# Loading the first two blocks of each rest chain earlier and thinner, with their tables built at twice the rate

## The chip, the cores and the metric

The kernel runs on one core of a Trainium2 chip. A core has a tensor engine (PE, with its weight loads shown apart as PEld), a vector engine (DVE), a scalar engine (ACT), GpSimd (POOL) and a sync engine (SP) that here does almost nothing but issue DMA transfers. Each engine works through its own list of instructions in order; semaphores hold one back for another. The metric is the time of one execution on the device in microseconds (us).

## The reference

`x` is 8 sequences of 5056 rows with 128 channels. First every channel of every sequence is convolved (linearly, along the rows) with a filter `h` of the same length, by real Fourier transforms of twice the length:

```python
Xf = np.fft.rfft(x, n=2*S, axis=1); Hf = np.fft.rfft(h, n=2*S, axis=0)
y = np.fft.irfft(Xf * Hf[None], n=2*S, axis=1)[:, :S, :]
```

The 40448 rows of the result are then the tokens of a mixture of 16 experts. A token's group is the largest of 4 group logits, its expert the largest of 4 logits in that group, and its weight is the product of the two softmax values. It goes through that expert alone:

```python
h = np.maximum(xg[mask_e] @ w1[g, e], 0.0)      # 128 -> 1024
out[tok_idx] = combined[:, None] * (h @ w2[g, e])   # 1024 -> 128
```

## The kernel before, in words

The convolution runs in three rounds over the sequences (`stage1`, `groups`, `side`), and the routed rows are scattered by expert into a table `srt` in DRAM. The experts then work on blocks of 512 rows of one expert. The first 59 blocks (`NW_MIN` = 59, numbered from 0) surely exist whatever the data, so they are written out without a branch: the plain blocks. Block 34 (`NA`) is the first for which all of the routing is known. What is left of each expert after that, the rest, depends on the data: some further blocks of 512 rows, then a chain of blocks of 384 rows (numbered from `T0` = 1000) and a chain of 256 rows (from `H0` = 2000), each block behind a branch.

One block is 8 steps. A step `k` of the plain blocks (k = 8 x block + step, 472 steps in all) has three matmuls of the first layer (`mm1`, L1400 to L1402: products of the high and low parts, into the PSUM tiles `px`/`aux`), a Relu on ACT (L1405), the low part of the hidden rows on DVE (L1406, `h0l` to `h3l`), and three matmuls of the second layer for an earlier step (L1418 to L1420). Between these lie the splits of the next block's weights and rows into high and low parts (`split`, ACT L1340 and DVE L1341), the turning of the next rows (L1356) and of the output (`out_turn`, L1459, up to block 51). Each split of the next block begins at step 4 of a block with the first half of its first weights, `w0h`.

The order of instructions is the order of the Python calls. For each step the loop in `run` calls `advance` on a few generators (a side chain's next piece) and then adds the step itself. Three of these matter here:

- `table_b` builds the three small tables that the rest needs (row and expert of each block): tens of DVE operations on 128x16 numbers, each piece ending in a `yield`, and for each table one store to DRAM (`tabd`, L1113) and one load back (`tabr`, L1118). It begins at step 272 (8 x `NA`).
- `fill_rows` writes 16 stretches of empty rows into `srt` (L1196), one every fourth step from step 284 on.
- `ffn_ahead` loads the first two blocks of each of the two chains, and then splits the first block's rows and weights into tiles of their own:

```python
for j in (T0, T0 + 1, H0, H0 + 1):
    yield from self.ffn_xs(j)          # four loads of rows (L1304), one of ids
    for q in (0, 2):
        self.ffn_w(j, (q,))            # one load of 512 KB of weights (L1333)
        yield
for j in (T0, H0):
    for q in ("x", 0, 1, 2) if j == T0 else ("x", 0, 1):
        self.keep_first(j, q)          # one split: ACT and DVE
        yield
        yield
```

So it has 28 pieces that issue a transfer and 14 that hold seven splits.

All of these transfers go through SP in program order, between the plain blocks' own: block j's step 0 issues the rows of block j+2 (L1304, four loads and the ids), step 2 its two weight loads (L1333), step 1 is followed by the store of the previous block's output (`outd`, L1460), and step 5 reads that output back row by row into the tile `xt` (`out_back`, L1465), which POOL then multiplies by the rows' weights (`weigh`, L1489, at step 1 of the next block) and scatters to the output (L1533). There is one such `xt` tile, so the read has to wait until POOL has weighed the rows before. `take` (L1465 too) reads back halves of outputs that earlier blocks had put aside.

Of the kernel before, what the change touches and what calls it, by code (L numbers as in the profile page):

```python
# [38 lines left out]
NW_MIN = NC  # L39
# [15 lines left out]
START1, END0 = 26, 24  # L55
NTA = 7
FILL, EMPTY = 12, 256
AHEAD = 52
RP = 3
PRE = 40  # L60
LOAD1 = 14
# [176 lines left out]
class Kernel:  # L238
# [1506 lines left out]
    def run(self):  # L1745
        tc = self.tc
        with ExitStack() as ctx:
            self.pools(ctx)
            with ExitStack() as c2:
# [10 lines left out]
                def add(f, w=0.0, ends=False):  # L1760
                    main.append((w, f, ends))
# [4 lines left out]
                def advance(g):  # L1766
                    return lambda: next(g, None)
# [47 lines left out]
                ta, tq, tb, fill = self.table_a(), self.table_c(), self.table_b(), self.fill_rows()  # L1815
                ahead = self.ffn_ahead()
                steps = [f for j in range(NW_MIN) for f in self.ffn_steps(j, (BLK, None) if j else None, NW_MAX)]
                for k, f in enumerate(steps):
                    for g in rest[LATE * k:LATE * k + LATE]:
                        add(g)  # L1820
                    if k == 8 * (N0 - 2) - SIDE1:
                        mark["end", 1] = len(main)
                    if k == START2 - 7:
                        add(lambda: [side[2][0](q) for q in range(len(SIDE_AT))])
                    if k == START2:
                        mark["start", 2] = len(main)
                    if 8 * (N0 - 2) - SIDE1 < k:
                        for _ in range(NTA):
                            add(advance(ta))
                    if k == 8 * (NA - 2) - SIDE2:  # L1830
                        mark["end", 2] = len(main)
                    if 8 * (NA - 2) - SIDE2 < k < 8 * NA:
                        for _ in range(NTA):
                            add(advance(tq))
                    if 8 * NA <= k:
                        add(advance(tb))
                    if 8 * NA + FILL <= k and k % 4 == 3:
                        add(advance(fill))
                    if 8 * NW_MIN - AHEAD <= k:
                        add(advance(ahead))  # L1840
                    if k < 4:
                        add(lambda q=(0, 2, 1, 3)[k]: self.ffn_w(1, (q,)))
                    add(f, FW[k % 8])
                    if k in (8 * (N0 - 2) - 1, 8 * (NA - 2) - 1):
                        add(self.drain)
                    elif k < 8 * (NA - 2) and k % 8 not in (3, 4, 5, 6):
                        add(lambda: self.send("s"))
                    elif k >= 8 * (NA - 2) and k % 8 in (7, 0, 1, 2):
                        add(lambda: self.scatter_out(1, True))
                    if k % 8 == 6:  # L1850
                        add(self.more_due)
                    m, n = k // 8 - NA, (PUT1 - PUT0) // 2
                    if k % 8 == 3 and 0 <= m < TAKE and (m + 1) * n // TAKE > m * n // TAKE:
                        add(lambda i=m * n // TAKE: self.take(i))
# [32 lines left out]
```

## Time and profile before

| | |
|---|---|
| runs before | 1615.23, 1625.37, 1626.6 us; median 1625.37 us |
| the profiled execution | 1622.21 us, its span 1620.5 us |
| granted PE clock over the span | 0.997 |
| busy: PE, DVE, ACT, POOL | 96%, 82%, 62%, 51% |
| DMA moved | 345.88 MB, 213 GB/s in the mean |

The span runs from the first to the last instruction that the profile shows; the run's time holds 1.7 us more. A busy share is a mean over the whole span, which has very different stages; the stage of this change is the part from about 1060 us (step 272) to 1340 us (end of the plain blocks). DVE and ACT intervals may overlap a little with the next one, since instructions are pipelined, so what an operation costs its engine is read from the distance of two starts.

### The profile page before, as it was taken

The page shows a single profiled execution, that of the slowest core. Times are in us where ns is not written, and L with a number is a line of the kernel's source. Part 1 is how long each engine was busy: PE and PEld are TensorE (multiplying, and loading weights), DVE is VectorE, ACT ScalarE, POOL GpSimd, SP SyncE. Part 2 cuts the span into 40 slices and gives each one's busy share as a digit, 9 for nine tenths or more (in the row PEclk, how much of TensorE's full clock was granted, in tenths as well). Part 3 has the DMA queues.
Part 4 walks back from the last instruction along what each step waited for, and adds up shares of the span by engine and source line. Part 5 has one row for each costly group of instructions (what it writes and reads, how often), then busy time and mean ns, then how long its engine had stood idle before and what let it go on. Part 6 is the DMA issues. An engine that isn't in the chain of part 4 may idle for free. (4 is left out here: it accounts for less than half of the span.)

```text
span 1620.5 us, 47337 instructions
## 1 busy us (share of the span) xinstructions
PE 1559.0 (96%) x16248; PEld 1217.5 (75%) x16248; DVE 1322.4 (82%) x2817; ACT 1001.6 (62%) x2240; POOL 827.3 (51%) x812
## 2 busy tenths in 40 slices
PE   8998999998899989999999999999999999999997
PEld 8676855557766647887777777788888877888997
DVE  6554699885698987888888889999998988887887
ACT  5565544444455546666666666677776777666775
POOL 1453234343375663155655666355777866234444
PEclk9999999999999999999999999999999999999999
DMA  7797879889799988667787757677888996555666
GB/s 213 217 293 241 229 230 285 274 245 244 195 276 304 293 222 227 177 180 193 193 201 202 197 158 184 181 201 213 222 226 229 241 254 171 130 139 152 158 176 171
DMA packets 431204, 345.88 MB, mean 213 GB/s; under 512 B 279964, under 2 KB 370593, under 8 KB 430936
## 3 DMA queue, kind: packets, MB, share of 16 engines
q1 hardware_dynamic: 410328, 300.80, 68.3%
q0 software_dynamic: 20608, 41.79, 7.8%
q8 instruction: 134, 2.20, 0.6%
q14 instruction: 134, 1.10, 0.2%
HBM read 239.32 MB, written 103.65 MB: 212 GB/s over the span
## 5 line engine op out<-in xcount | busy, mean ns | idle before, releaser
L878 POOL DMA_INDIRECT srt<-rw,pos x320 | 343.1, 1072 | 331.3 <-DVE y L552 66.4
L1533 POOL DMA_INDIRECT out<-orow,at x176 | 185.2, 1052 | 162.9 <-ACT at L1531 86.4
L552 DVE TENSOR_TENSOR y<-pp,hg 128x768 f32<-128x768 f32 (+1 forms) x120 | 103.3, 861 | 53.0 <-ACT hg L542 32.0
L1533 POOL DMA_INDIRECT out<-orow,sids x92 | 90.8, 987 | 103.2 <-DVE orow L1438 70.5
L612 ACT COPY zs<-pp 128x768 f32<-128x768 f32 (+1 forms) x118 | 85.2, 722 | 54.9 <-PE pp L602 36.4
L602 PE MATMUL pp<-y,cg 64*64 64x384 f32 (+1 forms) x1472 | 113.7, 440 | 5.6 <-DVE rw L995 3.6
L534 PE MATMUL pp<-st,cg 64*64 64x192 f32 (+1 forms) x1556 | 114.2, 404 | 2.0 <-PE pp L602 1.3
L1405 ACT ACTIVATE h0h<-px 128x512 fp32r<-128x512 f32 (+1 forms) x109 | 64.0, 587 | 79.7 <-PE px L1402 79.6
L447 DVE TENSOR_TENSOR st<-pp,odd 128x320 f32<-128x320 f32 x90 | 43.8, 487 | 75.4 <-ACT odd L446 74.9
L767 ACT COPY yT<-py 128x474 f32<-128x474 f32 (+1 forms) x96 | 44.3, 514 | 96.9 <-PE py L760 96.9
L552 DVE TENSOR_TENSOR m<-pp,hg 128x768 f32<-128x768 f32 (+1 forms) x120 | 103.0, 858 | 0.7 <-ACT te L932 0.7
L1406 DVE SCALAR_TENSOR_TENSOR h0l<-px,h0h 128x512 fp32r<-128x512 f32 (+1 forms) x109 | 72.9, 669 | 30.2 <-ACT h0h L1405 29.0
L1406 DVE SCALAR_TENSOR_TENSOR h3l<-px,h3h 128x512 fp32r<-128x512 f32 (+1 forms) x111 | 74.5, 671 | 24.3 <-ACT h3h L1405 22.9
L534 PEld LDWEIGHTS pp<-st,cg 64*64 64x64 f32 x1556 | 59.0, 133 | 43.9 <-issue 32.2
L1405 ACT ACTIVATE h2h<-px 128x512 fp32r<-128x512 f32 (+1 forms) x112 | 65.8, 587 | 40.0 <-PE px L1402 36.3
L586 POOL TENSOR_TENSOR y<-y,m 128x512 f32<-128x512 f32 x40 | 50.9, 1275 | 75.6 <-DVE m L574 42.5
L602 PEld LDWEIGHTS pp<-y,cg 64*64 64x64 f32 x1472 | 55.9, 133 | 44.3 <-issue 30.8
L1406 DVE SCALAR_TENSOR_TENSOR h2l<-px,h2h 128x512 fp32r<-128x512 f32 (+1 forms) x112 | 74.9, 669 | 13.8 <-ACT h2h L1405 11.2
L746 PEld LDWEIGHTS py<-ig,zm 126*64 126x64 f32 x2048 | 73.1, 137 | 14.6 <-issue 8.5
L746 PE MATMUL py<-ig,zm 126*64 126x79 f32 x2048 | 81.2, 235 | 2.6 <-DMA zm<-zd 2.6
L1405 ACT ACTIVATE h3h<-px 128x512 fp32r<-128x512 f32 (+1 forms) x111 | 65.2, 587 | 19.7 <-PE px L1402 15.9
L1405 ACT ACTIVATE h1h<-px 128x512 fp32r<-128x512 f32 (+1 forms) x111 | 65.2, 588 | 18.7 <-PE px L1402 16.0
(478 smaller groups left out, 5018.8 us busy)
## 6 DMA issues: line engine op xcount, KB each, us to landing
wr<-in_moe_w SPq DMA_DIRECT2D x186, 512.0 KB
zm<-zd SPq DMA_DIRECT2D x64, 378.0 KB
zd<-zs SPq DMA_DIRECT2D x62, 384.0 KB
cg<-in_c_g SPq DMA_DIRECT2D x102, 224.0 KB
xr<-srt SPq DMA_DIRECT2D x284, 64.0 KB
xt<-in_x SPq DMA_DIRECT2D x82, 160.0 KB
hg<-hd SPq DMA_DIRECT2D x80, 128.0 KB
zd<-zs SPq DMA_DIRECT2D x39, 256.0 KB
```

Source lines behind the costliest of these rows:

```text
L447: nc.vector.tensor_tensor(out=all_st[:, 0:2 * HALF, d], in0=even, in1=odd, op=ALU.add)
L534: nc.tensor.matmul(px[c * 64:c * 64 + 64, b, to], lhsT=k, rhs=data[:, of], start=begin, stop=i == len(steps) - 1 or p == 0 and i == 1, til ...
L552: self.mark["v"] = nc.vector.tensor_tensor(out=t[:, :, 0:w].rearrange("p t (r u d) -> p t r u d", r=2, u=nu), in0=taken(px, part).unsqueez ...
L586: self.mark["v"] = (nc.gpsimd if r == 0 else nc.vector).tensor_tensor(out=y[:, :, 0:w], in0=y[:, :, 0:w], in1=m[:, :, 0:w], op=ALU.add)
L602: nc.tensor.matmul(pz[c][h:h + 64, 0:w], lhsT=wt[c * 64:c * 64 + 64, k + h:k + h + 64], rhs=y[c * 64:c * 64 + 64, part, 0:w], start=part = ...
L612: self.mark["s"] = nc.scalar.copy(out=z[:, 0:n, 0:w], in_=pp[:, 0:n, 0:w])
L746: nc.tensor.matmul(pys[q][c:c + 64, col(n, u)], lhsT=zms[q][:, n % QB, k:k + 64], rhs=self.ig[:, 0:NH], start=n % QB == 0 and u == 0, stop ...
L767: nc.scalar.copy(out=self.yT[:, k:k + QB * c1], in_=pys.pop(q)[:, 0:QB * c1])
L878: ins = self.nc.gpsimd.indirect_dma_start(out=self.srt, out_offset=bass.IndirectOffsetOnAxis(ap=k["pos"][0:p, j:j + 1], axis=0), in_=k["rw ...
L1405: self.mark["s"] = nc.scalar.activation(out=hh, in_=p, func=AF.Relu)
L1406: nc.vector.scalar_tensor_tensor(out=hl, in0=p, scalar=0.0, in1=hh.bitcast(F32), op0=ALU.max, op1=ALU.subtract)
L1533: ins = self.nc.gpsimd.indirect_dma_start(out=self.a["out"], out_offset=bass.IndirectOffsetOnAxis(ap=ids, axis=0), in_=o, in_offset=None, ...
```

## The change

`table_b` is advanced twice a step instead of once. `ffn_ahead` is advanced from step 362 on (472 - 110) instead of step 420 on (472 - 52), and only at odd steps instead of at every step.

```diff
-AHEAD = 52
+AHEAD = 110
...
                     if 8 * NA <= k:
                         add(advance(tb))
+                        add(advance(tb))
                     if 8 * NA + FILL <= k and k % 4 == 3:
                         add(advance(fill))
-                    if 8 * NW_MIN - AHEAD <= k:
+                    if 8 * NW_MIN - AHEAD <= k and k % 2:
                         add(advance(ahead))
```

Step 363 is step 3 of block 45, so the 28 transfers stand at steps 363 to 417 instead of 420 to 447, and the seven splits at every fourth step from 419 on instead of every second from 448 on. Nothing is added or taken away.

On DVE, block 37 after its first weight split is a place in the middle of the tables. The names are the table's working tiles (`ge`, `ex`, `tt`, `sm`, `sel`); L1406 and L1341 are the block's own work. Before:

```order
L1341 TENSOR_TENSOR w0l<-wr_17558,w0h 128x512
L1090 TENSOR_SCALAR tt<-e_280,ex 128x16
L1406 SCALAR_TENSOR_TENSOR h1l<-aux,h1h 128x512
L1341 TENSOR_TENSOR x0l<-xturn,x0h 128x512
L1092 TENSOR_TENSOR sel<-to_17566,tt 128x16
L1406 SCALAR_TENSOR_TENSOR h2l<-px,h2h 128x512
L1341 TENSOR_TENSOR w2l<-wr_17560,w2h 128x512
L1094 TENSOR_REDUCE sm<-sel 128x1
```

and now, at the same splits of the same block:

```order
L1341 TENSOR_TENSOR w0l<-wr_17586,w0h 128x512
L1075 TENSOR_SCALAR ge<-cum,iop 128x16
L1077 TENSOR_REDUCE ex<-ge 128x1
L1406 SCALAR_TENSOR_TENSOR h1l<-aux,h1h 128x512
L1341 TENSOR_TENSOR x0l<-xturn,x0h 128x512
L1079 TENSOR_TENSOR tt<-ge,nt 128x16
L1081 TENSOR_REDUCE sm<-tt 128x1
L1406 SCALAR_TENSOR_TENSOR h2l<-px,h2h 128x512
L1341 TENSOR_TENSOR w2l<-wr_17588,w2h 128x512
L1083 TENSOR_SCALAR ex<-ex 128x1
L1085 TENSOR_TENSOR row<-iop,cum 128x1
```

Two table operations stand behind each split where one stood, and the tables are already at the second of the three. Over the whole of `table_b` it is 86 operations on DVE, spread over 114 steps before and over 57 now.

On SP, the place is step 2 to 5 of block 45: the second weight load of block 47, then the reads of block 44's output (`xt_138`, here `outd_119`) and of earlier ones (`take`), then the rows of block 48 (`xr_19249` before, `xr_19279` now; L1275 loads the block's row number into a register). Before:

```order
L1333 DMA wr_19144<-in_moe_w 128x1024
L1465 DMA take<-outd_89 128x4x64
L1465 DMA take<-outd_90 128x4x64
L1465 DMA xt_138<-outd_119 128x4x128
L1275 TENSOR_LOAD tabr_16674
L1275 ISA x2
L1304 ISA
L1304 DMA xr_19249<-srt 32x16x32
```

and now:

```order
L1333 DMA wr_19168<-in_moe_w 128x1024
L1275 TENSOR_LOAD tabr_18083
L1275 ISA x2
L1304 ISA
L1304 DMA xr_19183<-srt 32x12x32
L1465 DMA take<-outd_89 128x4x64
L1465 DMA take<-outd_90 128x4x64
L1304 ISA
L1304 DMA xr_19183<-srt 32x12x32
L1465 DMA xt_138<-outd_119 128x4x128
L1304 ISA
L1304 DMA xr_19183<-srt 32x12x32
```

The rows of block T0 (`xr_19183`) now go out between a plain block's weights, its reads of output and the next block's rows. So each of the next seven blocks has four of the 28 among its own transfers.

## Rows read from the trace of the kernel before

**Rows 1.** Busy time by stretch: tables and fills, steps 363 on, rest of plain blocks, rest

```profile
core 0: us, PE busy (x) PEld busy (x) DVE busy (x) ACT busy (x) POOL busy (x), PEclk, DMA share, GB/s
1060.00:1198.00 138.00, 137.27 (x606) 112.81 (x605) 133.95 (x267) 98.49 (x239) 86.90 (x89) 1.00 0.80 216
1198.00:1278.00 80.00, 79.71 (x353) 65.36 (x352) 73.24 (x120) 57.05 (x142) 65.11 (x63) 1.00 0.88 235
1278.00:1340.00 62.00, 60.07 (x269) 48.00 (x268) 53.83 (x87) 46.79 (x117) 44.42 (x46) 1.00 0.95 241
1340.00:1440.00 100.00, 99.95 (x449) 80.08 (x448) 82.57 (x147) 69.72 (x125) 42.49 (x44) 1.00 0.58 146
```

**Rows 2.** Who PE waited for, 1055 to 1345 us: total, times, longest

```profile
PE pz L1418 <- ACT h1h L1405: 1.4, 1, 1.4
PE px L1402 <- DVE x1l L1341: 0.7, 1, 0.7
```

**Rows 3.** DVE in time order: start us, us, instruction; first and last table operation included

```profile
1062.96 0.17 DVE L1213 TENSOR_TENSOR cntb<-base,base 128x16 f32<-128x16 f32 x1
...
1097.05 2.13 DVE L1341 TENSOR_TENSOR w1l<-wr,w1h 128x512 fp32r<-128x512 f32 x1
...
1104.25 0.23 DVE L1090 TENSOR_SCALAR tt<-e,ex 128x16 f32<-128x16 f32 x1
1104.39 0.68 DVE L1406 SCALAR_TENSOR_TENSOR h1l<-aux,h1h 128x512 fp32r<-128x512 f32 x1
1104.99 0.68 DVE L1341 TENSOR_TENSOR x0l<-xturn,x0h 128x512 fp32r<-128x512 f32 x1
1105.59 0.17 DVE L1092 TENSOR_TENSOR sel<-to,tt 128x16 f32<-128x16 f32 x1
1105.67 0.68 DVE L1406 SCALAR_TENSOR_TENSOR h2l<-px,h2h 128x512 fp32r<-128x512 f32 x1
...
1219.94 0.10 DVE L1252 CAST nbh<-cum 1x1 int32<-1x1 f32 x1
```

**Rows 4.** POOL in time order, the weighing beside the long split of rows 3

```profile
1097.56 1.06 POOL L1489 TENSOR_TENSOR orow<-xt,ids 128x512 f32<-128x512 f32 x1
```

**Rows 5.** DVE in time order: outputs of blocks 44, 47 and 51 turned

```profile
1186.67 0.71 DVE L1459 STREAM_TRANSPOSE oT<-pz 128x512 f32<-128x512 f32 x1
...
1219.31 0.71 DVE L1459 STREAM_TRANSPOSE xt<-ptr 128x512 f32<-128x512 f32 x1
...
1264.66 0.70 DVE L1459 STREAM_TRANSPOSE xt<-ptr 128x512 f32<-128x512 f32 x1
```

**Rows 6.** SP in time order: the stores of these three outputs issued

```profile
1195.79 0.56 SPq L1460 DMA_DIRECT2D outd<-oT  x1
...
1230.07 0.56 SPq L1460 DMA_DIRECT2D outd<-xt  x1
...
1267.62 0.44 SPq L1460 DMA_DIRECT2D outd<-xt  x1
```

**Rows 7.** ACT in time order: the first weight split that waited longest, two blocks

```profile
1236.09 0.62 ACT L1340 CAST w0h<-wr 128x512 fp32r<-128x512 f32 x1 [2.46 <-DMA wr<-in_moe_w]
...
1316.18 0.62 ACT L1340 CAST w0h<-wr 128x512 fp32r<-128x512 f32 x1 [3.62 <-DMA wr<-in_moe_w]
```

**Rows 8.** SP in time order: block T0 + 1 (three rows), then a plain block's rows

```profile
1285.40 2.36 SPq L1304 DMA_DIRECT2D xr<-srt  x4
1287.94 0.40 SPq L1304 DMA_DIRECT2D ids<-srt  x1
1289.13 0.81 SPq L1333 DMA_DIRECT2D wr<-in_moe_w  x1
1290.79 2.08 SPq L1304 DMA_DIRECT2D xr<-srt  x4
```

**Rows 9.** What SP waited for, 1195 to 1285 us: total, times, longest

```profile
SPq L1465 <- POOL orow L1489: 11.8, 6, 4.9
```

**Rows 10.** DMA queue's share and its issues by tile, 1340 to 1440 us

```profile
q1 hardware_dynamic: 26352, 11.84, 49.5%
...
wr<-in_moe_w SPq DMA_DIRECT2D x17, 512.0 KB
...
xr<-srt SPq DMA_DIRECT2D x36, 64.0 KB
```

## The prediction

> **What bounds the kernel now.** I began with the busy times by stretch, because a mean over the whole span hides the stage that the change touches. [rows 1] show PE busy in nearly all of every stretch from 1060 to 1440 us, at a granted clock of 1.00: it misses 0.73 us of the first 138, 0.29 of the next 80, 1.93 of the next 62, 0.05 of the last 100. So PE sets the time, and 3.0 us is about all that the change can win. Then I asked what PE waited for. [rows 2] name two waits of size: 1.4 us on a Relu of ACT and 0.7 us on the low part of a block's rows from DVE. The first leads to a late load: ACT works in order, and `w0h` stood there for 3.62 us until its weights had landed [rows 7]. The reader is to see two engines beside PE that have little left, and of different kinds. In 1060 to 1198 us DVE is busy 133.95 of 138 us; in 1278 to 1340 us the DMA engines are busy at 0.95, and at 0.88 already in 1198 to 1278 us, where the loads now go [rows 1].
>
> The pace to hold against is PE's: the outputs of blocks 44 and 47 are turned 32.64 us apart, which is 10.88 us a block and 1.36 a step [rows 5].
>
> **The tables, twice as dense.** The own work of a plain block on DVE is 15 large operations (8 low parts, 4 weight splits, one split of rows, two transposes), 0.60 us from start to start (1104.39 to 1104.99 and on to 1105.59) [rows 3], so 9.0 us. A table operation takes 0.14 and 0.08 us in the same way; I take 0.11. The 86 of them lie between 1062.96 and 1219.94 us [rows 3], 114 steps or 6.0 a block, 0.66 us. There is a third load: once a block POOL weighs a block's rows, and where that meets a split, the split takes 2.13 us instead of 0.68 [rows 3, 4]. That is 1.45 us a block at most and nothing at least; I take half, 0.7. Before, the sum is 10.4 us of 10.88, and DVE gets by. Now the 86 stand in 57 steps, 12.1 a block, 1.33 us, and the sum is 11.0 us: 0.15 us too much a block, for 7.1 blocks 1.1 us. With a full 1.45 us for the weighing it is 11.8 us, 6.4 us in all. The low part of a step is needed by PE only two steps later, so a little lateness costs nothing; one such wait of 0.7 us was left before. With nothing late enough the price is 0. I take 2.0 us, nearer to the small end, because DVE with 133.95 of 138 us busy lost only 0.7 us of PE before. In return no table operation is left after step 330, which is at about 1142 us, and the wait of 0.7 us for `x1l`, which came at 1160 us, should go: -0.7.
>
> [...]
>
> **The loads, in their new place.** Four blocks of rows and weights move from about 1270 to 1318 us to about 1198 to 1275 us. Two accounts bound what that costs.
>
> By DMA time: in 1340 to 1440 us the hardware queue was busy for 49.5 of 100 us with 36 loads of rows, that is 9 blocks of 512 rows, and their weights [rows 10]: 5.5 us a block. The four are of 384, 384, 256 and 256 rows with full weights, so they cost between 2.5 and 4 such blocks, 13.8 to 22 us. The 54 steps they are spread over last 73 us, and with a share of 0.88 taken there [rows 1] 9 us are free. So 5 to 13 us find no place and make what follows late.
>
> By SP's time: SP is late there already. The output of block 44 was turned by 1187.38 us and stored at 1195.79, 8.4 us late; of block 47, 10.05 us; of block 51, 2.3 us [rows 5, 6]. At 10 us of lateness the weights came 2.46 us late to ACT [rows 7] and PE lost 0.29 us [rows 1]; so 10 us is the limit from which lateness is paid by PE, and at the place of the first load 1.7 us of it are left. SP needs about 6.5 us to issue for one of the four: 2.36 and 0.40 for rows and ids, two weight loads of up to 0.81, and about 0.8 for each of three register loads, the gap ahead of 1289.13 [rows 8]; 26 us in all. Of that the 6.1 us may be taken off by which it caught up from block 44 to 51, and at best the 11.8 us in which it waited for POOL's weighing [rows 9]. So 18.2 us over the limit at worst, 6.4 if the waits are filled; by DMA time it is 3.3 to 11.3.
>
> I take 6.0 us: the waits get filled, since what SP waits for there is POOL and not a transfer, and the two accounts then overlap at 6 to 11; the lower end, because a PE that is held up also gives SP and the queue its time back. The 0.29 us lost there before is in it: -0.3.
>
> **The old place.** Without these transfers the stretch from 1278 us on has plain blocks alone, of the kind whose successors run at a share of 0.58 and lose 0.05 us in 100 [rows 1]. The 1.93 us should go: -1.9. The seven splits (1.2 us of ACT and DVE each by the starts of rows 3) move from every second to every fourth step, about 30 steps earlier; DVE is busy 53.83 of 62 us there [rows 1] and they then stand beside nothing else that is new, so 0. The chains themselves gain nothing: no row of [rows 2] or wait near their starts is for one of these loads. The waits that the change adds are those on SP: behind a waiting SP stand the next plain block's rows and weights, for which ACT waits, and the reads of output, for which POOL waits.
>
> **The sum.** +2.0 - 0.7 + 6.0 - 0.3 - 1.9 = +5.1 us. On the profiled execution, 1622.21 us (the span and 1.7 us around it), this gives 1627.3 us; on the median of the runs, which is 3.2 us above that execution, 1630.5 us. I say **1629 us**. The three runs before lie 11 us apart, 0.7%, so a change under 1%, 16 us, can hardly be told from none by them.
>
> **The rivals.** (a) *Everything is covered* (20%). DVE's lateness stays within the two steps, SP's waits for POOL swallow the loads, and lateness of the loads is not paid. For it: PE lost 0.29 us with SP 10 us late, and the loads are thinner by half, one at every second step. Against it: 13.8 us of transfers at least for 9 us of room. Then -0.7 - 0.3 - 1.9 = -2.9 us is left, 1619 to 1622.5 us. [...]
>
> (b) *A ring of SP, DMA and POOL* (10%), the case over 1% slower. The read of a block's output into the one `xt` tile waits for POOL's weighing, and the weighing waits for that read to land. If the loads between them delay the read, POOL weighs and scatters later, and it has little room to catch up (65.11 of 80 us busy [rows 1]); then SP's waits for POOL don't shrink, none of the 11.8 us is won, and 18.2 us are paid. With the tables at 4 us and the gains of 2.9 that is +19.3 us, 1641 to 1645 us. It decides from the point where the weighing starts later in its block than before.
>
> (c) *The change doesn't do what it says* (3%): the first of these loads is held on SP until the last fill has landed, which was issued seven steps before it, and everything behind it stands. That would add one wait of a few us to the forecast, 1632 us.
>
> **How the numbers follow.** The forecast has 67%, (a) 20%, (b) 10%, (c) 3%. The forecast's own range, with the table term from 0 to 6.4 and the loads from 3.3 to 11.3, is +0.4 to +14.8 on the mean of both bases (1623.8), 1624 to 1639. To hold 8 in 10 I reach into (a) and up to (b)'s edge: 1618 to 1641. Over 1% slower is (b) and the upper edge of the forecast, 11%; over 1% faster has no row behind it, 2%; within 1%, 87%.
>
> **What would show it.** In the profile after: the last table operation (`nbh`) at about 1143 us instead of 1219.94; DVE without a pause between two table bursts, and PE waits on L1406 or L1341 before 1145 us of about 2 us. SP's stores of blocks 46 to 51 more than 10 us after their turning, `w0h` waiting for `wr` by 3 us and more in several blocks between 1200 and 1290 us, and PE missing 4 to 8 us in that stretch. From then to the end of the plain blocks no wait of `w0h`, and a DMA share of 0.7 or less. I am wrong if PE misses under 1.5 us from 1198 to 1290 us (then the limit on SP's lateness was misread), or if the plain blocks end more than 12 us later (then the ring is at work).

## The result, and the profile after

| | before | changed |
|---|---|---|
| runs | 8 | 8 |
| median, us | 1620.78 | 1632.44 |
| lowest to highest, us | 1615.23 to 1631.17 | 1628.44 to 1635.03 |
| the profiled execution, us | 1622.21 (span 1620.5) | 1633.71 (span 1632.0) |

The ratio of changed to before is 1.0068, with a 95% interval of 1.0046 to 1.009. The change makes the kernel slower by about 11 us. The forecast was +5.1 us, 1629 us, with a range of 1618 to 1641: the sign and the range held, the size was half of what came. That 1629 us lie only 3.4 us below the measured median is in part luck: the three runs on which the forecast was built have a median of 1625.37 us, 4.6 us above that of all eight.

First the busy time by stretch of the changed kernel, columns as in [rows 1], with five microseconds of their own at the end:

```profile
1060.00:1198.00 138.00, 137.03 (x603) 112.35 (x602) 129.54 (x275) 97.42 (x238) 87.71 (x87) 1.00 0.80 217
1198.00:1278.00 80.00, 73.49 (x305) 57.00 (x304) 63.75 (x97) 48.05 (x121) 57.05 (x57) 0.98 0.88 238
1278.00:1340.00 62.00, 60.94 (x272) 48.41 (x271) 56.22 (x88) 46.85 (x118) 48.82 (x48) 1.00 0.89 234
1340.00:1440.00 100.00, 100.00 (x450) 80.33 (x449) 82.78 (x145) 70.38 (x133) 44.83 (x46) 1.00 0.56 138
1270.00:1275.00 5.00, 4.71 (x13) 3.45 (x14) 5.00 (x8) 3.53 (x9) 2.29 (x3) 0.68 0.85 172
```

One stretch has changed: from 1198 to 1278 us, where the 28 transfers now stand, PE misses 6.51 of 80 us where it missed 0.29. The count of matmuls says more than the busy time: 305 where there were 353, 48 fewer at 0.227 us each (80 us by 353), or 10.9 us. A matmul that runs at a lower clock counts as busy for longer, so a busy share hides part of a loss: in the last row, at a granted clock of 0.68, 13 matmuls make 4.71 us busy, 0.36 us each. The DMA share in that stretch is 0.88, as before.

Who PE waited for, 1055 to 1345 us, columns as in [rows 2]:

```profile
PE ptr L1418 <- ACT h1h L1405: 4.2, 3, 2.8
PE pz L1418 <- ACT h1h L1405: 2.5, 2, 1.6
PE pz L1420 <- DVE h1l L1406: 1.0, 1, 1.0
PE pz L1420 <- DVE h3l L1406: 0.4, 1, 0.4
```

`h1h` is the Relu of ACT that stands behind the split of `w0h`, the case of [rows 7]. ACT in time order shows it, one split of `w0h` per block, with its wait in brackets:

```profile
1203.93 0.62 ACT L1340 CAST w0h<-wr 128x512 fp32r<-128x512 f32 x1 [0.71 <-DMA wr<-in_moe_w]
1215.85 0.62 ACT L1340 CAST w0h<-wr 128x512 fp32r<-128x512 f32 x1 [1.74 <-DMA wr<-in_moe_w]
1229.00 0.62 ACT L1340 CAST w0h<-wr 128x512 fp32r<-128x512 f32 x1 [3.79 <-DMA wr<-in_moe_w]
1241.64 0.62 ACT L1340 CAST w0h<-wr 128x512 fp32r<-128x512 f32 x1 [3.37 <-DMA wr<-in_moe_w]
1254.02 0.62 ACT L1340 CAST w0h<-wr 128x512 fp32r<-128x512 f32 x1 [3.07 <-DMA wr<-in_moe_w]
1269.03 0.62 ACT L1340 CAST w0h<-wr 128x512 fp32r<-128x512 f32 x1 [5.12 <-DMA wr<-in_moe_w]
1280.51 0.61 ACT L1340 CAST w0h<-wr 128x512 fp32r<-128x512 f32 x1
1294.06 0.62 ACT L1340 CAST w0h<-wr 128x512 fp32r<-128x512 f32 x1 [2.41 <-DMA wr<-in_moe_w]
1305.55 0.62 ACT L1340 CAST w0h<-wr 128x512 fp32r<-128x512 f32 x1
```

Four blocks in a row wait 3 to 5 us, where one waited 2.46 before, and the wait of 3.62 us further on [rows 7] has gone.

The waits are late loads, and the loads are late on SP. DVE in time order, the outputs of blocks 47 and 51 being turned:

```profile
1221.97 0.70 DVE L1459 STREAM_TRANSPOSE xt<-ptr 128x512 f32<-128x512 f32 x1
...
1276.31 0.70 DVE L1459 STREAM_TRANSPOSE xt<-ptr 128x512 f32<-128x512 f32 x1
```

and SP in time order, the stores of these two being issued:

```profile
1236.00 0.43 SPq L1460 DMA_DIRECT2D outd<-xt  x1
...
1286.41 0.37 SPq L1460 DMA_DIRECT2D outd<-xt  x1
```

From the end of a turning to the issue of its store, SP is 13.3 us late at block 47 (10.05 before) and 9.4 at block 51 (2.3 before) [rows 5, 6]. Block by block it is 10.0, 12.4, 13.3, 12.7, 13.2, 12.4 and 9.4 us from block 45 to 51. Before, SP caught up from block 47 on, 6.6 us at block 49 and 2.3 at block 51; now it stays at 12 to 13, which is where ACT's waits begin to hold PE, and with it everything that would be later still.

What SP does in that time, in time order around the longest wait:

```profile
1266.25 0.50 SPq L1465 DMA_DIRECT2D xt<-outd  x1
1266.95 5.89 SPq L1304 DMA_DIRECT2D xr<-srt  x5
1273.04 0.40 SPq L1304 DMA_DIRECT2D ids<-srt  x1
1273.62 0.36 SPq L1304 DMA_DIRECT2D xr<-srt  x1
1274.08 0.39 SPq L1460 DMA_DIRECT2D outd<-oT  x1
```

The row of 5.89 us holds more than five issues: between a rest block's load and the four of a plain block lie the register load and the address steps, which this view does not list. The five issues themselves take 0.38, 0.78, 0.74, 1.72 and 0.71 us. All loads of rows from 1198 to 1278 us, the duration of one issue in ns (least, median, most), now and then before:

```profile
L1304 SPq DMA_DIRECT2D xr<-srt x40: 332/563/1722, 1201.8 to 1276.5; - x40
L1304 SPq DMA_DIRECT2D xr<-srt x33: 316/564/2863, 1200.7 to 1277.9; - x33
```

So one load costs SP no more than it did (one of a plain block 0.65 us in the mean now and 0.64 before); there are more of them. The wait of SP for POOL, 11.8 us in [rows 9], has gone from 1195 to 1285 us altogether; the longest that is left there is this one, columns as in [rows 9]:

```profile
SPq L1304 <- ACT at L1531: 0.9, 1, 0.9
```

So SP has next to nothing left to wait for. Its issues between 1198 and 1278 us, added up one by one, take 41.7 us before (83 of them) and 47.7 us now (91); the rest is register loads, address steps and gaps. Of the gaps longer than 0.3 us there were eight before, 12.6 us in all, and there are two now, of 0.36 us each: SP is full. The 28 transfers with their register loads, each counted from the end of the issue ahead of it to its own end, take SP 25.7 us in the old place and 25.7 us in the new one.

How much of the 11 us each part makes is read from starts of the same instruction in both traces. The output of block 32 is turned at these times, before and then now, DVE in time order:

```profile
1054.74 0.71 DVE L1459 STREAM_TRANSPOSE oT<-pz 128x512 f32<-128x512 f32 x1
1056.48 0.70 DVE L1459 STREAM_TRANSPOSE oT<-pz 128x512 f32<-128x512 f32 x1
```

So 1.7 us are there already ahead of the change, and are taken off in what follows. At block 43 (1176.34 and 1177.66) nothing is lost, at block 45 0.9 us, at block 51 9.9. Then the splits of `w0h`, ACT in time order, before:

```profile
1278.40 0.61 ACT L1340 CAST w0h<-wr 128x512 fp32r<-128x512 f32 x1
...
1301.09 0.62 ACT L1340 CAST w0h<-wr 128x512 fp32r<-128x512 f32 x1
```

and now, of the splits behind those listed above:

```profile
1316.67 0.61 ACT L1340 CAST w0h<-wr 128x512 fp32r<-128x512 f32 x1
1328.01 0.61 ACT L1340 CAST w0h<-wr 128x512 fp32r<-128x512 f32 x1
```

The split that stood at 1278.40 stands at 1294.06, 13.9 us late. The one that stood at 1301.09 stands at 1316.67, 13.8 us late. The next stood at 1316.18 [rows 7] and stands at 1328.01, only 10.1 us late, because it waited 3.62 us before and does not now. From there on it stays at 10.3.

### The profile page after: what moved, and what is told of

It is laid out like the page before. It is cut to its first block, busy times and chain, and to the rows that moved or that the text cites. A ratio compares the mean times of both kernels' runs of the same rounds, so it can differ in the third digit from the quotient of the medians.

```text
span 1632.0 us, 47346 instructions
## 1 busy us (share of the span) xinstructions
PE 1569.4 (96%) x16248; PEld 1221.7 (75%) x16248; DVE 1318.6 (81%) x2817; ACT 997.6 (61%) x2240; POOL 828.6 (51%) x812
## 5 line engine op out<-in xcount | busy, mean ns | idle before, releaser
L1533 POOL DMA_INDIRECT out<-orow,at x176 | 185.8, 1055 | 162.8 <-ACT at L1531 86.9
L1405 ACT ACTIVATE h0h<-px 128x512 fp32r<-128x512 f32 (+1 forms) x109 | 63.9, 586 | 75.7 <-PE px L1402 75.7
L1406 DVE SCALAR_TENSOR_TENSOR h0l<-px,h0h 128x512 fp32r<-128x512 f32 (+1 forms) x109 | 72.6, 666 | 26.6 <-ACT h0h L1405 25.7
L1406 DVE SCALAR_TENSOR_TENSOR h3l<-px,h3h 128x512 fp32r<-128x512 f32 (+1 forms) x111 | 74.3, 669 | 24.1 <-ACT h3h L1405 22.9
L586 POOL TENSOR_TENSOR y<-y,m 128x512 f32<-128x512 f32 x40 | 50.8, 1275 | 77.0 <-DVE m L574 42.5
L1405 ACT ACTIVATE h2h<-px 128x512 fp32r<-128x512 f32 (+1 forms) x112 | 65.6, 585 | 38.3 <-PE px L1402 34.9
L746 PE MATMUL py<-ig,zm 126*64 126x79 f32 x2048 | 84.3, 239 | 3.2 <-DMA zm<-zd 3.2
L746 PEld LDWEIGHTS py<-ig,zm 126*64 126x64 f32 x2048 | 76.0, 141 | 15.3 <-issue 8.2
L1406 DVE SCALAR_TENSOR_TENSOR h2l<-px,h2h 128x512 fp32r<-128x512 f32 (+1 forms) x112 | 74.6, 666 | 13.7 <-ACT h2h L1405 11.6
L1341 DVE TENSOR_TENSOR w0l<-wr,w0h 128x512 fp32r<-128x512 f32 x88 | 61.7, 701 | 20.2 <-ACT w0h L1340 20.1
L1405 ACT ACTIVATE h1h<-px 128x512 fp32r<-128x512 f32 (+1 forms) x111 | 65.1, 586 | 19.0 <-PE px L1402 16.9
```

What stands on the lines that cost most here:

```text
L586: self.mark["v"] = (nc.gpsimd if r == 0 else nc.vector).tensor_tensor(out=y[:, :, 0:w], in0=y[:, :, 0:w], in1=m[:, :, 0:w], op=ALU.add)
L746: nc.tensor.matmul(pys[q][c:c + 64, col(n, u)], lhsT=zms[q][:, n % QB, k:k + 64], rhs=self.ig[:, 0:NH], start=n % QB == 0 and u == 0, stop ...
L1341: (eng or nc.vector).tensor_tensor(out=l, in0=src, in1=h.bitcast(F32), op=ALU.subtract)
L1405: self.mark["s"] = nc.scalar.activation(out=hh, in_=p, func=AF.Relu)
L1406: nc.vector.scalar_tensor_tensor(out=hl, in0=p, scalar=0.0, in1=hh.bitcast(F32), op0=ALU.max, op1=ALU.subtract)
L1533: ins = self.nc.gpsimd.indirect_dma_start(out=self.a["out"], out_offset=bass.IndirectOffsetOnAxis(ap=ids, axis=0), in_=o, in_offset=None, ...
```

## The experiments

Kernels of one set ran on the same chip and are compared with the kernel before on that chip. The second and third set ran on other chips, on which the kernel before itself needs 1753.78 and 1755.84 us, so only ratios can be held against the first set's. "Lateness" is always that of SP as above, from the end of a turning to the issue of its store. On those two chips SP is late earlier: in the traced execution of every kernel with the denser tables it is at its worst 10.6 to 13.7 us late in blocks 40 to 43, ahead of the first of the 28 transfers, and `w0h` waits up to 4.7 us there. In late_three_of_four, with the tables as before, it is at most 6.1 us late there, and no `w0h` waits. So the ratios of these two sets may hold a cost of the tables as well.

| kernel | median, us | before there, us | ratio | 95% interval |
|---|---|---|---|---|
| tables_alone | 1620.47 | 1619.51 | 1.0005 | 0.9986 to 1.0023 |
| loads_alone | 1630.5 | 1619.51 | 1.0065 | 1.004 to 1.0091 |
| two_read_tiles | 1628.21 | 1619.51 | 1.0062 | 1.0045 to 1.0079 |
| weights_early_rows_late | 1631.44 | 1619.51 | 1.0088 | 1.0057 to 1.0118 |
| changed_again | 1760.62 | 1753.78 | 1.0039 | 1.0013 to 1.0066 |
| rows_early_weights_late | 1759.42 | 1753.78 | 1.0021 | 0.9995 to 1.0048 |
| loads_from_act | 1756.69 | 1753.78 | 1.0019 | 0.9992 to 1.0045 |
| small_loads_added | 1770.14 | 1753.78 | 1.0085 | 1.0055 to 1.0116 |
| sp_from_380 | 1759.85 | 1755.84 | 1.003 | 1.0005 to 1.0054 |
| act_from_380 | 1753.23 | 1755.84 | 0.9986 | 0.9962 to 1.0011 |
| sp_from_390 | 1754.86 | 1755.84 | 1.0004 | 0.9979 to 1.003 |
| late_three_of_four | 1749.88 | 1755.84 | 0.9976 | 0.9946 to 1.0005 |

### Each half of the change alone

**tables_alone** is the kernel before with only the tables made denser:

```diff
                     if 8 * NA <= k:
                         add(advance(tb))
+                        add(advance(tb))
```

> The tables at two operations a step, the loads where they were before. Theory: -1 to +2 us on before, since the shift between the two traces at the end of the table stage is about that of its beginning. Rival (tables carry the loss): +5 to +9 us. In both, SP late by some 3 us more than before at blocks 40 to 43.

Measured: 1.0005, no difference. Its busy time by stretch, columns as in [rows 1]:

```profile
1060.00:1145.00 85.00, 84.41 (x371) 68.87 (x370) 83.38 (x202) 60.60 (x145) 48.98 (x49) 1.00 0.76 205
1060.00:1198.00 138.00, 137.34 (x604) 112.71 (x604) 132.97 (x277) 98.05 (x238) 88.54 (x88) 1.00 0.80 218
1198.00:1278.00 80.00, 80.00 (x356) 66.28 (x355) 74.80 (x110) 58.64 (x144) 66.37 (x65) 1.00 0.89 241
```

DVE is busy 83.38 of 85 us while the tables are built, and PE misses 0.59 us in them; but over 1060 to 1198 us it misses 0.66, against 0.73 in [rows 1]. The loss has moved forward and is not larger. SP does feel the tables: its lateness is 5.0 us at block 36, where it was 0.0, and 8.1 to 8.8 at blocks 40 to 42 instead of 5.5 to 5.9. From block 44 on it is as before or less.

**loads_alone** is the other half:

```diff
-AHEAD = 52
+AHEAD = 110
...
-                    if 8 * NW_MIN - AHEAD <= k:
+                    if 8 * NW_MIN - AHEAD <= k and k % 2:
```

> The loads in their new place, the tables at one operation a step as before. If the loads among the output-reading blocks are the cause (theory): +8 to +12 us on before, ratio 1.005 to 1.0075, w0h waiting for wr by 3 us and more in blocks 46 to 52. If the denser tables carry the loss, by DVE or by making SP late sooner (rival): +2 to +5 us.

Measured: 1.0065, all of the loss of the whole change (1.0068). Its stretch of the loads:

```profile
1198.00:1278.00 80.00, 73.33 (x300) 57.48 (x299) 61.66 (x107) 47.47 (x118) 54.64 (x54) 0.96 0.89 231
```

PE misses 6.67 us, as in the changed kernel. The lateness rises to 15.6 us at block 48, and `w0h` waits 2.98, 5.62, 1.68 and 4.5 us from block to block. What the tables do to SP at blocks 36 to 42 therefore adds nothing that can be told: the loads alone cost as much.

### The ring through the one read tile

**two_read_tiles** is the changed kernel with a second tile for the read of outputs, so that a read need not wait until POOL has weighed the rows before:

```diff
-        t = self.xt[4][:, 0:now * D].rearrange("p (a m c) -> p a m c", a=4, c=SQ)
+        t = self.xt[(4, 1)[j % 2]][:, 0:now * D].rearrange("p (a m c) -> p a m c", a=4, c=SQ)
```

> The changed kernel with two tiles in turn for the read of a block's output, so that SP no longer has to wait there until POOL has weighed the rows before. If the loss is a ring of SP, DMA and POOL (rival): 4 to 8 us faster than the changed kernel, +3 to +7 us on before. If the loads simply find no room in DMA time (theory): within 2 us of the changed kernel, +9 to +12 us on before.

Measured: 1.0062, with the lateness still at 9.7 to 13.1 us in blocks 45 to 50 and `w0h` waiting 3.23, 2.56, 3.81 and 4.1 us. The profiled execution is 5.9 us late at block 51 where the changed kernel's is 9.9, but by the medians the two cannot be told apart. The ring is at most a small part.

### Which of the transfers

**weights_early_rows_late** leaves only the eight weight loads at odd steps from 363 on, where they now follow each other (to step 377), and takes the 20 loads of rows and ids back to step 420:

```diff
...
         for j in (T0, T0 + 1, H0, H0 + 1):
-            yield from self.ffn_xs(j)
+            self.blk[j] = {}
             for q in (0, 2):
                 self.ffn_w(j, (q,))
                 yield
+
+    def ffn_ahead2(self):
+        for j in (T0, T0 + 1, H0, H0 + 1):
+            yield from self.ffn_xs(j)
...
+                    if 8 * NW_MIN - 52 <= k:
+                        add(advance(ahead2))
```

> The changed kernel with only the eight weight loads (4.2 of 4.8 MB) in the new place, from step 363 on; the rows and ids (20 of 28 transfers, short pieces) go from step 420 on, one a step. If bytes are what finds no room: +7 to +11 us on before. If the number of transfers on SP or the short pieces do: 0 to +4 us.

Measured: 1.0088, no better than the whole change. By the expectation this speaks for the bytes. But the eight loads stand closer together here than in the change, over 15 steps instead of 54. Its busy time by stretch:

```profile
1195.00:1225.00 30.00, 27.26 (x113) 21.77 (x112) 22.98 (x36) 18.35 (x46) 22.85 (x23) 0.95 1.00 299
1225.00:1278.00 53.00, 50.78 (x223) 41.45 (x222) 45.62 (x69) 35.60 (x88) 38.70 (x40) 1.00 0.92 247
```

This is another way to lose: eight loads of 512 KB in some 20 us put the DMA engines at 1.00, SP's lateness jumps to 16.0 us at block 46 and is gone by block 51 (1.1), and two waits of `w0h` (4.92 and 4.4 us) make most of the loss.

**rows_early_weights_late** is the opposite: the 20 loads of rows and ids at odd steps from 363, the weights from step 420, by the same two generators with their contents exchanged.

```diff
         for j in (T0, T0 + 1, H0, H0 + 1):
             yield from self.ffn_xs(j)
+
+    def ffn_ahead2(self):
+        for j in (T0, T0 + 1, H0, H0 + 1):
             for q in (0, 2):
                 self.ffn_w(j, (q,))
...
```

> The changed kernel with rows and ids (20 of 28 transfers, 0.65 MB in short pieces) in the new place and the eight weight loads (4.2 MB) from step 420 on, one a step. If the bytes of the weights are what finds no room: -1 to +4 us on before. If each transfer costs alike: +6 to +10 us.

Measured: 1.0021 on a chip where the whole change gives 1.0039, so the two can't be told apart there, nor this one from before, and it decides between neither expectation. The lateness is 7.8 to 10.5 us from block 44 to 50, at the limit, and the waits of `w0h` stay below 1.8 us in the new place; one of 2.75 us stands in the old place.

**changed_again** is the changed kernel unaltered, to have it on that chip. 

> The changed kernel once more, beside the three that follow: +9 to +13 us on before (1.0055 to 1.008).

 Measured: 1.0039, less than expected, with the same signs (lateness 8.0 to 13.2 us in blocks 46 to 50, waits of `w0h` of 3.62 and 5.51 us).

### SP's time or the DMA engines' time

**loads_from_act** lets ACT issue the same 28 transfers at the same steps, with their register loads:

```diff
+        eng = nc.scalar if j in (T0, T0 + 1, H0, H0 + 1) else nc.sync
-        rb = nc.sync.value_load(
+        rb = eng.value_load(
...
-            ins = nc.sync.dma_start(out=out.unsqueeze(1), in_=src)
+            ins = eng.dma_start(out=out.unsqueeze(1), in_=src)
...
-                nc.sync.dma_start(out=t.unsqueeze(1), in_=w[q // 2][:, bass.ds(e, 1)])
+                eng.dma_start(out=t.unsqueeze(1), in_=w[q // 2][:, bass.ds(e, 1)])
```

> The changed kernel with the 28 transfers and their register loads issued by ACT instead of SP, at the same steps. If what runs out is SP's time for issuing (theory of SP's account): +1 to +5 us, w0h waits under 2 us. If it is the transfers' time on the DMA engines (theory of the DMA account): within 3 us of the changed kernel, +8 to +13 us, since the same bytes pass the same engines.

Measured: 1.0019, not to be told from before, nor from changed_again. SP's lateness falls to 2.8 us at block 46 and 0.0 at blocks 47 and 48, and no `w0h` waits from 1300 us on. In its place came a wait of another kind. What ACT waited for, 1300 to 1400 us:

```profile
ACT h3h L1407 <- DMA srt<-none: 10.0, 1, 10.0
```

The first load of rows has to wait until the last of the empty rows are in `srt` (L1407 is L1405 of the other kernels). SP, itself 13.4 us late at block 44, issues those only at 1297.4 us. In changed_again this wait does not show, because SP issues the last empty rows at 1293.7 us and comes to the first load of rows at 1304.46. The wait holds PE too (its longest in this stretch, 7.8 us, is for that `h3h`), and this gives SP time to catch up. So the fall of the lateness here is not the work of the issuing engine alone. Its DMA queues, 1300 to 1400 us, columns as in [rows 10] (q1 holds SP's transfers, q10 ACT's):

```profile
q1 hardware_dynamic: 37650, 16.95, 65.8%
q10 hardware_dynamic: 7872, 4.86, 20.1%
```

The four blocks' loads cost 20.1 us of the sixteen engines.

**act_from_380** does the same from step 381 on, late enough for the empty rows to have landed, and **sp_from_380** issues at those same steps from SP:

```diff
-AHEAD = 110
+AHEAD = 92
```

> The changed kernel with the 28 transfers issued by ACT and begun at step 381 instead of 363, so that the fills have landed before the first read of sorted rows. If SP's time was what ran out: -3 to +2 us on before, SP late by less than 6 us at blocks 48 to 51 and no plain block's w0h waiting over 1 us. If the transfers' 20 us of DMA time don't fit in either case: +6 to +11 us.

> The same start at step 381, but issued by SP as in the changed kernel: the control for the run from ACT. 18 of the 28 stand among blocks that read their output back, instead of 28. Theory: +4 to +9 us on before.

Measured: 0.9986 from ACT and 1.003 from SP, 1753.23 and 1759.85 us, with intervals that overlap a little (0.9962 to 1.0011 and 1.0005 to 1.0054). Busy time of act_from_380:

```profile
1300.00:1400.00 100.00, 94.16 (x394) 73.24 (x393) 82.46 (x123) 64.31 (x165) 76.64 (x76) 0.98 0.94 250
```

and of sp_from_380:

```profile
1300.00:1400.00 100.00, 92.96 (x392) 72.76 (x390) 78.86 (x121) 62.02 (x159) 73.15 (x72) 0.98 0.85 232
```

With ACT issuing, the DMA engines take 0.94; with SP, only 0.85. PE is equally far along in both (394 and 392 matmuls), so this stretch does not show where the 6.6 us between the medians are lost. ACT's waits there, act_from_380:

```profile
ACT w0h L1342 <- DMA wr<-in_moe_w: 2.6, 2, 1.7
```

and sp_from_380:

```profile
ACT w0h L1340 <- DMA wr<-in_moe_w: 17.7, 8, 4.8
```

From SP, the lateness stays at 11.6 to 13.3 us in blocks 47 to 51; from ACT it falls, 7.1, 4.7, 2.3, 3.5 and 0.0. The two waits of `w0h` with ACT issuing (1310 and 1320 us) lie ahead of the first of the 28, at 1321.5 us. The same bytes at the same steps: what differs is who spends the time to issue them.

**small_loads_added** should charge SP without the bytes: tables_alone, and at the 28 odd steps from 363 on a load of 2 KB with the same three register loads in seven, while the real loads stay at their old place.

```diff
...
+                if i in (0, 5, 6):
+                    e = nc.sync.value_load(tab[0:1, 2 * k:2 * k + 1], min_val=0, max_val=NE - 1)
+                t = self.fx.tile([128, 4], F32, name="small", bufs=4)
+                nc.sync.dma_start(out=t.unsqueeze(1), in_=w[:, bass.ds(e, 1), 0:4])
+                yield
...
```

> The kernel with the tables alone changed (the loads in their old place), and in addition 28 loads of 2 KB each at the odd steps from 363 on, with three register loads to every seven, as the real ones have: SP's work of the change without its bytes. They fill a tile that nobody reads. If SP's time runs out: +6 to +12 us on before. If DMA time does: 0 to +3 us.

Measured: 1.0085, by the medians a larger loss than the changed kernel's on that chip. The small loads take SP 25.9 us, counted as above, nearly as much as the real ones (27.9 us in changed_again). Yet in their own stretch little is lost: PE is busy 95.29 of 100 us from 1300 to 1400 us with 407 matmuls, against 92.51 with 383 in changed_again, and no `w0h` waits from 1300 to 1395 us. But SP is still 10.3 us late at block 51, and then the real loads come. Busy time there:

```profile
1390.00:1460.00 70.00, 55.22 (x213) 42.03 (x212) 43.09 (x70) 35.59 (x91) 39.10 (x39) 0.88 0.73 191
```

PE misses 14.78 of 70 us at a DMA share of 0.73, with `w0h` waiting 5.85 and 5.99 us. Not all of that belongs to the loads: PE misses 9.60 us of the same 70 in changed_again and 10.56 in late_three_of_four, where no `w0h` waits. So this run does not show that SP's work without the bytes is enough for the loss. In the place of the change it was not, in this one execution; the loss came where the real loads met an SP that was already late.

### Fewer blocks that read outputs

**sp_from_390** starts at step 391, in block 48, where SP before was catching up:

```diff
-AHEAD = 110
+AHEAD = 82
```

> The changed kernel begun at step 391 (13 of 28 among those blocks). Theory: the loss goes with the number that stand there: +2 to +6 us on before. A loss that stays at +9 to +12 us would speak for the thinning or the tables and against the place.

Measured: 1.0004, under the range expected. The lateness is 0.0 to 3.3 us in blocks 46 to 51, and no `w0h` waits there. This execution says less than that sounds. It lost some 7 us of PE between blocks 45 and 48 (39.99 us between the splits of `w0h` at 1295.04 and 1335.03, against 32.97 for the same two in sp_from_380), so SP had caught up (0.03 us at block 47) before the first of the 28, at 1338.04 us. By the medians the loss shrinks with a later start: 363 costs 1.0039, 381 costs 1.003, 391 nothing that shows (the first on another chip than the others). The intervals overlap, so the order is not shown.

**late_three_of_four** is the kernel before, started eight steps earlier and leaving out every fourth step:

```diff
-AHEAD = 52
+AHEAD = 60
...
-                    if 8 * NW_MIN - AHEAD <= k:
+                    if 8 * NW_MIN - AHEAD <= k and k % 4 != 3:
```

> The kernel before with the loads begun at step 412 instead of 420 and advanced at three steps of four: nearly all behind the blocks that read their output back, somewhat thinner. Theory: -3 to +1 us on before, w0h waits of block 56 under 3.62 us.

Measured: 0.9976, with no wait of `w0h` in any plain block and a lateness of 0.0 to 2.1 us in blocks 46 to 51. It is the fastest of all, but its interval ends at 1.0005, so a gain is not shown.

## Why the prediction was right in direction and too small in size

**What bounds the kernel: right.** PE sets the time, and the limit from which SP's lateness is paid, read as 10 us from one wait [rows 6, 7], held roughly: of the five blocks that are 12 to 13 us late in the changed kernel four wait 3 to 5 us and the fifth not at all; waits of up to 1.8 us come already at 9.2 us; in tables_alone, with at most 8.8, none in the stretch waits more than 0.5; in rows_early_weights_late, at 7.8 to 10.5, the waits are 1 to 2 us or none.

**The tables: +2.0 - 0.7 forecast, about 0 measured.** The tables end where forecast. DVE in time order, the last table operation:

```profile
1144.79 0.13 DVE L1252 CAST nbh<-cum 1x1 int32<-1x1 f32 x1
```

A PE wait of 1.0 us for DVE (`h1l`) came with them, half of the 2 us forecast, and the wait for `x1l` went. The lower end of the term was right, and both signs came, but they cancel: tables_alone gives 1.0005 on that chip. By the two traces nothing is lost up to block 43.

**The loads in their new place: +6.0 - 0.3 forecast, about +14 measured.** This is the step that failed, as a size. It set the price by "the lower end, because a PE that is held up also gives SP and the queue its time back", where the accounts ran from 3.3 to 18.2. The traces show none of that time coming back. Three things in it were off.

- The 9 us of room were not to be had. They stood on a DMA share of 0.88 that would rise to 1.0. It stayed at 0.88 (0.89 in loads_alone) while PE missed 6.5 us. When ACT issued, on the two other chips, the same loads brought the share to 0.94 and 0.96, where issued from SP they left it at 0.85 and 0.87. So what ran out first was SP's time, not the engines'. The account by DMA time was the wrong one to lean on; the upper end of its cost, 22 us of the engines for the four blocks, was near the 20.1 measured.
- The account by SP's time, 6.4 to 18.2 us, held 14. Its price was right: 26 us for the four blocks, and SP spent 25.7. The waits for POOL were filled, as forecast, which is worth 11.8. The 13.9 us that remain come out at what PE lost by this pair of traces. Wrong was to take off the 6.1 us of catching up as well, and 1.7 us up to the limit: SP stayed at 12 to 13 us to block 50. Wrong too was the step from there to the lower end.
- One wait cost more than its own length, if what came behind it is put down to it. After PE had stood for 2.81 us behind the wait of 5.12, the granted clock was 0.68 in 1270 to 1275 us. PE in time order:

```profile
1267.09 0.39 PE L1402 MATMUL aux<-x1l,w1h 128*128 128x512 f32 x1
1270.29 0.50 PE L1418 MATMUL ptr<-h1h,w3h 128*128 128x512 f32 x1 [2.81 <-ACT h1h L1405]
...
1271.85 0.63 PE L1402 MATMUL px<-x0l,w0h 128*128 128x512 f32 x1
1272.27 0.63 PE L1418 MATMUL ptr<-h2h,w3h 128*128 128x512 f32 x1
...
1275.24 0.40 PE L1419 MATMUL ptr<-h3h,w3l 128*128 128x512 f32 x1
1275.47 0.40 PE L1420 MATMUL ptr<-h3l,w3h 128*128 128x512 f32 x1
```

Starts that are otherwise 0.23 us apart are 0.42 apart here; from 1271.85 to 1275.24 us the granted clock was 0.51. The eight from 1271.85 to 1275.24 took 3.39 us instead of 1.84, which is 1.55 us on top of the wait.

**The old place: -1.9 forecast, -3.7 measured.** The wait of 3.62 us went, as forecast. PE had lost that wait in full by the starts of `w0h`, while the busy time of [rows 1] showed only 1.93. Not all of it was due to the loads: in tables_alone, which has them in the old place too, the same split waits 0.99 us, so part of the gain is the chance of one execution. The sign for it, no wait of `w0h` after 1290 us and a DMA share of 0.7 or less, failed in both parts: one wait of 2.41 us at 1294, still caused by the moved loads, whose last go out at about 1288 us, and a share of 0.89 from 1278 to 1340 us. Plain blocks without the loads need more there than the 0.58 of the blocks behind them.

**The rivals.** (a), everything covered, did not come: the change does cost. How far the DMA engines were from full is read from two more runs: their share is 0.94 at 250 GB/s (act_from_380, 1300 to 1400 us) and 1.00 at 299 (weights_early_rows_late, 1195 to 1225 us), against 0.88 at 238 in the changed kernel. (b), the ring, did not come as described: SP's waits for POOL did vanish, and a second tile changes nothing that shows by the medians. Its sign, the plain blocks ending more than 12 us later, was close: 12.0 us by the starts of `w0h`, 10.3 without the 1.7 from ahead of the change. (c), a held first load, did not come on SP, but its condition is real: from ACT the first load waited 10.0 us.

What carries the loss is shown up to SP: the loads alone make it, SP has no wait left in their place, and the weights that it issues late hold ACT and then PE. That it is SP's issuing, and not the bytes, rests on one pair, act_from_380 and sp_from_380, whose intervals overlap a little; small_loads_added, in its one traced execution, speaks against SP's work being enough without the bytes. What issuing from ACT saved is SP's time and not the transfers' own: from 1300 to 1400 us q1 and q10 of loads_from_act together took 85.9 us of the sixteen engines for 21.81 MB, 3.94 us per MB, and q1 of changed_again, where SP issues all of them, 78.2 us for 19.80 MB, 3.95 us per MB (by the same account act_from_380 has 3.92 and sp_from_380 3.80). By the medians of act_from_380 and sp_from_380 the saving is not small: from ACT 0.9986, from SP 1.003.

**What stays open.** How the 14 us divide between SP's own work and what the bytes add to it was not separated: small_loads_added was meant for that and added its cost to another place. An issue does not always take SP the same time: from 1300 to 1400 us the rows of SP's time order that hold four loads of rows, with the address steps between them, take 2.52 to 5.50 us in act_from_380 (eight such rows) and 2.56 to 3.77 us in sp_from_380 (six). Whether that comes from the load on the DMA engines or from a second engine that issues is not shown. Why the loss is 1.0039 on one chip and 1.0068 on another is open too; the intervals overlap.

## What to carry to other kernels

An engine that only issues transfers has a budget too (here SP's gaps longer than 0.3 us fell from 12.6 us in 80 to 0.7): take its lateness, from the instruction that a transfer waits for to its issue, block by block, and put more work on it only where that lateness is small or falling. Spreading transfers thinner did not help here, where it spread them into blocks in which the issuer was already late (10.05 us at block 47 before); a share of the DMA engines below 1 was no room (it stayed at 0.88 while PE missed 6.51 of 80 us). Price the added issues with their register loads, take off the waits that they fill, and take off nothing more: here 25.7 less 11.8 us came out as what PE lost.

## What the runs showed of the hardware that was not expected

- One issue of a load of rows held SP for 0.33 to 1.72 us within the same 80 us of the changed kernel, with no wait named in the trace. In weights_early_rows_late, from 1195 to 1225 us, where the DMA engines were busy at 1.00, the weight loads of 512 KB took 0.33 to 0.36 us to issue, and the loads of rows and ids beside them 0.56 to 2.36.
- A pause of PE of 2.81 us was followed by about 3.4 us at a granted clock of 0.51, which cost 1.55 us more. The other long waits of `w0h` in that stretch were not followed by this: the granted clock is 1.00 from 1198 to 1265 us, and its mean of 0.98 from 1198 to 1278 us is what those five microseconds at 0.68 give by themselves. In loads_alone it is 0.96.
- Two other chips ran the kernel before in 1753.78 and 1755.84 us, 8% longer than the first. PE's longest groups of waits there were put down to "issue": in changed_again 11.4 us in 24 times in the matmuls of L429 and 11.4 us in 31 times in those of L746, where the kernel before on the first chip has 7.7 us in 7 times for L429 and none of size for L746.
